# Casting DMAs on GpSimd's queue in place of casts on the engines, in an attention and MLP kernel

One core of a Trainium2 chip. The metric is the device time of one execution in microseconds (us), lower is better. A run more than 1.5% above the fastest of its kernel is called slow and left out of the ratios.

## The reference, cut to what matters

```python
# q, k, v: (4 batches, 8 heads, 768 positions, 64); n_sink = 4, window = 128
scores = q @ k.T / 8, kept where the key is one of the first 4 or within the window of 128
x   = softmax(scores) @ v                    # heads side by side: (4, 768, 512)
a1  = alpha1 * x + beta1
tok = w_tok @ a1                             # w_tok: (768, 768), over positions
u   = x + lam * tok
a2  = alpha2 * u + beta2
out = u + lam * (relu(a2 @ w_ch1) @ w_ch2)   # w_ch1: (512, 2048), w_ch2: (2048, 512)
```

All inputs are fp32; the products run in fp16.

## The kernel before

The program is a list of tasks. A planner in Python with estimated costs puts them in a fixed order on each engine and gives them buffers. Each engine then works through its own list in that order: a task that waits holds all that stand behind it. Batch 0's attention runs first, alone (the startup); then the MLP of batch b runs on TensorE beside the attention of batch b+1.

All loads are on SyncE's one queue, as fp32, and an engine casts each to fp16. A row below is one contiguous piece of the source; a load moves many of them:

```python
def load_qk(p, b, hp, t, wait=None):            # rows of 6 x 64 fp32 = 1536 bytes
    src = (q, k)[t][b, 2 * hp : 2 * hp + 2].rearrange("h (p r) d -> p h (r d)", p=P)
    done["nat", b, hp, t] = add(p, {SP: 480}, lambda e: nc.sync.dma_start(bf.t, src), ...)

def load_v0(p, G, r):                           # batch 0's v: rows of 64 fp32 = 256 bytes
    done["v0", G, r] = add(p, {SP: 520}, lambda e: nc.sync.dma_start(
        bf.t[:, sl], v[0, 4*G : 4*G+4, r*P : (r+1)*P, :].rearrange("h p d -> p h d")), ...)
# load_wtok: 6 loads with rows of 3072 bytes; load_w1, load_w2: rows of 2048 bytes into 4 staging buffers
...
# the order on SyncE's queue
for hp, t in QK_ORDER[:4]: load_qk(at(), 0, hp, t)
for r in range(2):         load_v0(at(), 0, r)
for hp, t in QK_ORDER[4:]: load_qk(at(), 0, hp, t)
... the rest of v0, then w_tok, w_ch1, lam, batch 1's q/k, w_ch2, batch 1's v
...
# casts: q/k on VectorE and GpSimd, v on GpSimd (one on ScalarE), w_tok on ScalarE and GpSimd,
# w_ch1 on ScalarE and GpSimd (8 each); w_ch2 is multiplied by lam on VectorE or GpSimd
# row sums of w_tok (for beta1): 36 small matmuls with a column of ones
```

The softmax here doesn't subtract the row's maximum and nothing guards it: scores larger than these inputs give would overflow.

## Time and profile before

| | before |
|---|---|
| median of three (lowest to highest) | 273.24 us (272.65 to 274.75) |
| span of the profiled run | 272.6 us |
| first MLP matmul of batch 0 | 44.0 us |
| first token product of batch 1 | 102.7 us |
| first MLP matmul of batch 1 | 112.4 us |

The three moments cut the run into a startup (44.0 us), the MLP stage of batch 0 (58.7), a gap in which batch 1's token product and its transposes run (9.7) and the rest (160.2). Each is the start of the first matmul of its group in TensorE's timeline (the prediction has the first at 43.8, read from the groups by window).

From the view of the DMA issues: how many loads of which size, and at the end the median us from issue to landing:

```profile
v<-in_v_dram SPq DMA_DIRECT2D x12, 128.0 KB, 4.7
```

From the page's 40 slices: the clock granted to TensorE in tenths (9 is 90% or more), never lowered.

```profile
PEclk9999999999999999999999999999999999999999
```

### The profile page before, as it was taken

How to read it: one execution, taken by the hardware profiler on the slowest of the kernel's cores; microseconds unless marked ns; L12 is line 12 of the kernel's file. 1: busy time of each engine (PE TensorE's matmuls, PEld its weight loads, DVE VectorE, ACT ScalarE, POOL GpSimd, SP SyncE). 2: the span in 40 equal slices, each digit the busy share in tenths (PEclk: the TensorE clock that was granted, in tenths of full speed). 3: DMA queues.
4: the chain of work that ended last, by engine and by line, in shares of the span. 5: the costliest groups of instructions: out<-in, count | busy, mean ns of one | idle time of the engine just before them, and what ended most of it. 6: DMA issues, size and time to landing. Idle time of an engine off the chain costs nothing.

```text
span 272.6 us, 4969 instructions
## 1 busy us (share of the span) xinstructions
PE 259.3 (95%) x1941; PEld 142.5 (52%) x1941; DVE 144.4 (53%) x292; ACT 129.9 (48%) x213; POOL 115.5 (42%) x139
## 2 busy tenths in 40 slices
PE   7799999996899999799999999999999999999994
PEld 7644756653454544355655444555654445665441
DVE  5565744776989925438895143379853333100222
ACT  1778936786741102688740024787700145773000
POOL 5649957820395895106988700004846000000000
PEclk9999999999999999999999999999999999999999
DMA  6999999999999536779978523100001223000221
GB/s 226 324 245 357 374 291 258 274 357 234 254 284 212 149 108 173 173 165 218 219 145 175 165 77 96 59 2 0 2 38 43 96 84 93 0 0 2 77 77 77
DMA packets 85838, 42.28 MB, mean 155 GB/s; under 512 B 73515, under 2 KB 77619, under 8 KB 85814
## 3 DMA queue, kind: packets, MB, share of 16 engines
q1 hardware_dynamic: 85792, 41.95, 57.4%
q8 instruction: 15, 0.25, 0.4%
q14 instruction: 9, 0.07, 0.1%
q10 hardware_dynamic: 22, 0.01, 0.0%
HBM read 30.16 MB, written 6.29 MB: 134 GB/s over the span
## 4 chain that ended last, share of the span: by engine, by line
PE 68%; DMA 17%; DVE 7%; SPq 4%; POOL 2%; issue 1%; ACT 1%; POOLq 0%; DVEq 0%; ACTq 0%
PE ch L808 29%; PE h L784 24%; PE tok L701 9%; DMA wst_w<-in_moe_w_ch_dram 6%; DMA nat<-in_q_dram 5%; DMA lb_b<-in_moe_beta_dram 3%; SPq L364 3%; DVE w2f L683 3%; PE pv L570 3%; PE S L523 2%; DVE E L547 2%; DMA wtn<-in_moe_w_tok_dram 2%; POOL w1f L228 1%; PE pv L563 1%; POOL n L228 1%
## 5 line engine op out<-in xcount | busy, mean ns | idle before, releaser
L784 PE MATMUL h<-uT,w1f 128*128 128x384 f16 x512 | 90.5, 326 | 2.7 <-DVE uT L730 1.5
L808 PE MATMUL ch<-w2f,hT 128*128 128x512 f16 x384 | 88.7, 379 | 0.5 <-DVE w2f L683 0.5
L784 PEld LDWEIGHTS <-w1f 128*128 128x128 f16 x512 | 47.7, 98 | 36.2 <-issue 7.0
L808 PEld LDWEIGHTS <-hT 128*128 128x128 f16 x384 | 36.3, 98 | 41.8 <-issue 1.4
L790 ACT ACTIVATE hT<-h 128x384 f16<-128x384 f32 x95 | 46.1, 492 | 19.9 <-PE h L784 18.2
L538 ACT ACTIVATE E<-S 128x1024 f16<-128x1024 f32 (+1 forms) x42 | 40.7, 1003 | 14.0 <-PE pv L570 8.6
L819 DVE TENSOR_TENSOR x<-x,ch 128x512 f32<-128x512 f32 x24 | 16.5, 686 | 52.2 <-PE ch L808 51.6
L612 POOL TENSOR_TENSOR tmp<-x,la_b 128x512 f32<-128x512 f32 x18 | 25.8, 1435 | 42.5 <-DVE x L594 42.4
L226 ACT CAST u<-x 128x512 f16<-128x512 f32 x20 | 12.3, 618 | 61.7 <-DVE x L710 61.7
L701 PE MATMUL tok<-xh,wtokT 128*128 128x512 f16 x144 | 34.4, 379 | 0.0
L228 POOL CAST n<-nat 128x768 f16<-128x768 f32 x28 | 25.2, 914 | 16.7 <-DMA nat<-in_q_dram 12.8
L710 DVE TENSOR_TENSOR x<-x,tok 128x512 f32<-128x512 f32 x24 | 16.4, 687 | 23.6 <-PE tok L701 18.6
L615 POOL TENSOR_TENSOR xh<-tmp,lb_b 128x512 f16<-128x512 f32 x18 | 25.0, 1389 | 0.7
L792 DVE TENSOR_SCALAR hT<-h 128x384 f16<-128x384 f32 x33 | 18.3, 554 | 11.4 <-PE h L784 11.0
L547 DVE TENSOR_TENSOR E<-E,maskn 128x1024 f16<-128x1024 f16 x25 | 24.2, 997 | 0.0
L701 PEld LDWEIGHTS <-wtokT 128*128 128x128 f16 x144 | 13.9, 98 | 16.1
L594 DVE TENSOR_TENSOR x<-pv,rec 128x256 f32<-128x256 f32 x48 | 20.4, 425 | 1.7
L570 PE MATMUL pv<-vf,E 128*128 128x65 f16 x328 | 18.2, 194 | 3.1 <-DVE E L547 2.2
L570 PEld LDWEIGHTS <-E 128*128 128x128 f16 x328 | 15.2, 97 | 9.3 <-DVE E L547 2.8
L683 DVE TENSOR_TENSOR w2f<-wst_w,lam_b 128x512 f16<-128x512 f32 x15 | 12.5, 870 | 3.6 <-DMA wst_w<-in_moe_w_ch_dram 3.5
L228 POOL CAST u<-x 128x512 f16<-128x512 f32 x4 | 2.5, 626 | 27.9 <-DVE x L710 27.9
L228 POOL CAST vf<-vnat 128x512 f16<-128x512 f32 x18 | 10.7, 616 | 7.7 <-DMA vnat<-in_v_dram 7.2
(94 smaller groups left out, 206.3 us busy)
## 6 DMA issues: line engine op xcount, KB each, us to landing
wst_w<-in_moe_w_ch_dram SPq DMA_DIRECT2D x16, 512.0 KB, 8.1
nat<-in_q_dram SPq DMA_DIRECT2D x16, 384.0 KB, 6.1
nat<-in_k_dram SPq DMA_DIRECT2D x16, 384.0 KB, 9.0
out_dram<-x SPq DMA_DIRECT2D x24, 256.0 KB, 2.0
vnat<-in_v_dram SPq DMA_DIRECT2D x18, 256.0 KB, 4.5
wtn<-in_moe_w_tok_dram SPq DMA_DIRECT2D x6, 384.0 KB, 5.7
v<-in_v_dram SPq DMA_DIRECT2D x12, 128.0 KB, 4.7
uT<-u SPq DMA_TRANSPOSE x18, 2.3
```

Of the source, the lines that this page charges most:

```text
L228: engine[e].tensor_copy(o, i)
L538: nc.scalar.activation(eT.t, pS.t[:, :, 0 : n * w].rearrange("p e (i w) -> p e i w", i=n), AF.Exp, scale=scale)
L547: nc.vector.tensor_mul(ev, ev, m.to_broadcast(list(ev.shape)))
L570: nc.tensor.matmul(po.t[:, hl, :], eT.t[:, e_, off + i, c : c + P], vf[j][:, h, :], start=(r < 2 and n == 0), stop=(n == len(parts) - 1 an ...
L594: nc.vector.tensor_mul(bx.t[:, 4 * G : 4 * G + 4, :], po.t[:, :, 0:D], rec.t.to_broadcast([P, 4, D]))
L612: nc.gpsimd.tensor_mul(tmp.t, bx.t.rearrange("p h d -> p (h d)"), la1_b)
L615: nc.gpsimd.tensor_add(bh.t, tmp.t, lb1_b)
L683: lambda e, a=a, src=src: engine[e].tensor_mul(w2f[:, a, :], src.t[:, a % 2, :], lam_b),
L701: nc.tensor.matmul(pt.t, wtokT[:, si, ti * P : (ti + 1) * P], hs[si].t, start=(si == 0), stop=(si == NR - 1 and b > 0))
L784: nc.tensor.matmul(ph.t, w1f[:, c, fi * P : (fi + 1) * P], bu.t[:, c, chk * NTOK : (chk + 1) * NTOK], start=(c == 0), stop=(c == NC - 1))
L790: nc.scalar.activation(bh.t[:, fi, :], ph.t, AF.Relu)
L808: nc.tensor.matmul(pc.t, bh.t[:, fi, nt * P : (nt + 1) * P], w2f[:, fi, :], start=(fi == 0), stop=(fi == NF - 1))
```

## The change

The intent: a DMA that GpSimd issues changes the type on the way. So q/k of batches 0 and 1, w_tok and w_ch1 arrive as fp16, and some 40 casts go. Row sums of w_tok become a reduction and a diagonal matrix, lam and beta1 are spread by small matmuls in place of broadcast loads, and the constants become planned tasks. SyncE's queue keeps v, w_ch2 and the later batches. The core of the diff:

```diff
+    def cast_qk(p, b, t, hps, wait=None):
+        src = (q, k)[t][b, 2*hps[0] : 2*hps[0] + n].rearrange("h (p r) d -> p h (r d)", p=P)
+        a = load(p, POOL, 530 + 50*n, lambda e: nc.gpsimd.dma_start(at_(bf)[:, lo:lo+n], src), ...)   # fp16 bf
     def load_wtok(p, ti, n):
-            nc.sync.dma_start(bf.t[:, ti % 3, :], moe_w_tok[ti*P : (ti+1)*P, :])
+            nc.gpsimd.dma_start(wt16.t[:, ti:ti+n, :], moe_w_tok[ti*P : (ti+n)*P, :]...)
     def load_w1(p, i):
-        for c in range(0, NC, 2): load_w(...)            # staging, cast later
+        nc.gpsimd.dma_start(w1f[:, :, i*512 : (i+1)*512], moe_w_ch1[:, i*512 : (i+1)*512]...)
...
-    for hp, t in QK_ORDER[:4]: load_qk(at(), 0, hp, t)   # and v0, w_tok, w_ch1 ..., all on SyncE
+    for hps in ((0,), (1,), (2, 3)):                     # on GpSimd's queue, first of all
+        for t in range(2): cast_qk(-10000 + 12*hps[0] + t, 0, t, hps)
+    g = gate(at(), done["c16", 0, 0, 0], ...)            # SyncE: after the first q piece
+    for G in range(2):
+        for r in range(NR): load_v0(at(), G, r, g)
+    for ti in range(0, NR, 2): load_wtok(-9000 + ti, ti, 2)
+    for i in range(2): load_w1(-8000 + 100*i, i)
+    ... batch 1's q/k (four casting DMAs), the other two of w_ch1
+    g = gate(at(), done["w1", 0], ...)
+    ... on SyncE: batch 1's v, w_ch2
```

GpSimd thus issues batch 0's q/k, w_tok, w_ch1 and batch 1's q/k without a break.

## The prediction

> **What bounds the kernel now.** I read four views, in this order. First the chain that ended last, in order of time:
>
> ```profile
> 1.81 5.61 DMA nat<-in_q_dram
> 7.44 0.37 SPq L337
> ...
> 31.48 9.19 DMA lb_b<-in_moe_beta_dram
> 40.72 0.09 issue
> 40.81 0.70 POOL lb_b L859
> 41.51 5.29 DMA wst_w<-in_moe_w_ch_dram
> 46.85 0.61 POOL w1f L228
> ...
> 58.12 6.67 DMA wst_w<-in_moe_w_ch_dram
> 64.81 1.29 DVE w2f L683 x2
> ...
> 227.21 20.80 PE h L784 x128
> 248.01 20.73 PE ch L808 x96
> 268.84 0.69 DVE x L819
> ```
>
> From about 85 us to 268.8 us the chain is TensorE alone: nothing that the change touches can shorten that stretch except by starting it earlier. Before 85 us it is DMA landings, casts on GpSimd and w2 products on VectorE. The chain's last stretch also gives the true price of a matmul: 20.80 us / 128 = 162.5 ns for 384 columns, 0.423 ns a column.
>
> Second, the groups by shape, with TensorE's counts in windows. PE's 95% busy hides waiting, so I multiplied the columns in each window by 0.423 ns (half for the half-array products S, a quarter for the sink products):
> - 0 to 43.8 us (the first MLP matmul starts there): 25.8 us of work, 18 us lost.
> - 43.8 to 102.85 us (MLP of batch 0 beside attention of batch 1): 52.0 us in 59.05, 7.0 lost, 4.9 of them between 60 and 80.
> - 170 to 227 us (the same stage, batch 2): 55.7 us in 57.0, 1.3 lost.
> So at most the 18 us and some 5.7 us are to be had.
>
> Third, durations of what goes and what stays:
>
> ```profile
> L228 POOL CAST n<-nat 128x768 f16<-128x768 f32 x28 | 25.2, 914 | 16.7 <-DMA nat<-in_q_dram 12.8 <-DVE w2f L683 2.6 <-DMA nat<-in_k_dram 1.2
> ...
> L683 DVE TENSOR_TENSOR w2f<-wst_w,lam_b 128x512 f16<-128x512 f32 x15 | 12.5, 870 | 3.6 <-DMA wst_w<-in_moe_w_ch_dram 3.5
> ...
> L603 POOL TENSOR_TENSOR xh<-x,la_b 128x256 f16<-128x256 f32 x12 | 8.5, 728 | 4.6 <-DVE rec L593 3.8 <-DVE x L594 0.5 <-PE S L523 0.2
> ...
> L228 POOL CAST w1f<-wst_w 128x512 f16<-128x512 f32 x8 | 4.9, 613 | 3.8 <-DMA wst_w<-in_moe_w_ch_dram 3.8
> L228 POOL CAST vf<-v 128x256 f16<-128x256 f32 x11 | 4.3, 408 | 0.8 <-DMA v<-in_v_dram 0.7
> ```
>
> Columns: count, busy us, mean ns, idle before. Fourth, the windows of 2 us, for the DMA's rate (last column, GB/s): q/k run at 300 to 360, the v loads with their 256-byte rows at about 210, w_tok and w_ch1 at 345 and more.
>
> ```profile
> 4.00:6.00 2.00, 2.00 (x22) 2.00 (x21) 1.57 (x3) 0.00 (x0) 0.59 (x2) 1.00 0.96 310
> ...
> 16.00:18.00 2.00, 2.00 (x22) 0.83 (x19) 1.05 (x2) 1.75 (x3) 0.87 (x3) 1.00 1.07 226
> ...
> 24.00:26.00 2.00, 2.00 (x29) 1.04 (x29) 0.56 (x2) 1.98 (x3) 1.82 (x5) 1.00 1.01 345
> ```
>
> The share of the DMA engines (the column before) is about 1 from 2 us on: in the first 40 us data comes as fast as it can, and a cast on the way doesn't lessen what is read.
>
> **What the Trainium skill says.** (1) "DMA: Bandwidth & Descriptors", Anatomy of one DMA: a GpSimd-issued transfer carries some 2.0 us of fixed cost. No run of before shows one; SP's first q load, issued at 0.80 us, is being cast at 3.95 us, so the first landing should differ little. (2) Same page, Queues, rings and completion order: the queues share the 16 engines, which take turns packet by packet. The trace agrees as to the sharing only in that one queue alone already fills the engines (share about 1). (3) "TensorEngine Tiling (Array Packing)", Key Properties and Restrictions: changing the tiling mode drains TensorE, and column tiling disables fast weight load. Before: eight S products take 0.54 us where their columns make 0.43, so a visit to another mode costs 0.1 us. (4) "SBUF — State Buffer", Who interferes with whom: VectorE in a two-port mode can starve GpSimd's descriptor writing. Not shown by before; most descriptors are written in the first 5 us, when VectorE only does memsets.
>
> **The change, part by part.**
> - *Casts gone.* 12 of the GpSimd n casts (0.82 us each, 9.9), 4 on VectorE (2.7), the six of w_tok (ACT 3.1, POOL 1.6), sixteen of w_ch1 (ACT 4.9, POOL 4.9). GpSimd loses 16.4 us, ScalarE 8.0. The 36 rs matmuls go too (36 x 128 columns, 1.9 us of PE), and the broadcast loads of lam and beta1, with the wait of 3.3 us on GpSimd for the latter.
> - *Added.* Row sums (three on ScalarE, three on VectorE, 0.8 us each by the cast of the same width), six small diagonals, one more spread copy.
> - *A new wait on GpSimd.* In the changed kernel's instruction order GpSimd issues fifteen DMAs ahead of any other work except the selects; from the ninth on each waits for the DMA eight earlier to land (they share eight semaphores; before shows SP held the same way, its load at 7.44 us released by the q landing at 7.42). The fifteenth waits for the seventh, the first w_tok piece. Call its landing T. Until T GpSimd casts no v, and PE in its fixed order stops at the sink-v product, ahead of the second head group's scores.
> - *T.* q/k of batch 0, 8 x 384 KB = 3.15 MB at 325 GB/s: 9.7 us; w_tok's first piece 0.79 MB at 350: 2.2 us; start about 2.3 us (estimate: first issue at 0.8 as in before, descriptors, first byte). That is 14.2. v of batch 0, 1.57 MB at 210, is 7.5 us and shares the engines from about 5 us on (it is held only until the first q piece). If it gets half the time or more it is all in front of T: 21.7. If it gets a small share, T is near 16. I take 19.
> - *From T to the MLP.* GpSimd: last issue 0.7, 11 v casts x 0.408 = 4.5, two row products x 1.25 = 2.5, 12 xh x 0.728 = 8.7: T + 16.4. ScalarE's second-group exps with three row sums among them end at about T + 12, so GpSimd leads. Then TensorE still has 34 of the 42 token matmuls x 0.216 us = 7.3. First MLP matmul at T + 24 = 43 us, against 43.8: the startup gains 0.8 us, not more, although so many casts went.
> - *MLP of batch 0.* w_ch1 needs no buffer and no cast; w_ch2's loads start when the first w_ch1 piece has landed (about T + 8), not after 47 us; VectorE does 10 rather than 15 of its products, and most before batch 1's masks. So the loss of 4.9 us between 60 and 80 should mostly go. Against it: the 8 q/k transposes of batch 1 are now 12 half-width matmuls each rather than 6. If column halves run side by side, as the four sink products do (0.33 us for what would be 0.87), that costs only drains, 4 visits x 0.1; if not, 8 x 0.33 = 2.7. I take 1.7. Batch 1's second half of q/k waits for buffers, so its scores start after 28 of 32 MLP-1 tiles rather than 17; I leave 1.5 us of stall. 52.0 + 1.3 + 1.7 + 1.5 = 56.5, against 59.05: 2.5 us gained.
> - *After.* Batches 1 to 3 keep their work: 0.
> Sum: -0.8 - 2.5 = -3.3 us: 273.2 becomes about 269.5 (rounded down a little, since GpSimd's freed time should help somewhere).
>
> **Rivals.** (A) The new queue takes v's place: T near 15 to 16, startup gains 4 us, half-width transposes are free, stalls gone: 264. For it: v's rows are 256 bytes, q's 1536, so turns taken descriptor by descriptor favour q. Against: turns may be by larger packets. (B) GpSimd becomes the bound of the startup: T at 22, first MLP matmul at 46, and what the MLP stage gains is just given back: 272 to 274. For it: the sum above needs only the v loads ahead of w_tok. (C) Casting transfers move slower than plain ones: 10% on the 5.5 MB ahead of T is 1.5 us, half the rate 12 us: up to 282. Nothing in the trace speaks for it; none is there to look at. (D) The late start of batch 1's attention leaves GpSimd's xh (6 x 2.8 us) and 8 casts (7.3 us) too little time before the token product: about 24 us from 72 us on, to 96, where TensorE arrives at about 100. Narrow; 1 to 3 us if missed.
>
> **Range and chances.** T moves the result one for one between 16 and 22 (-4 to +2 about the middle), the MLP stage by 2 either way: 263.5 to 275.5. Over 2% faster means under 267.8, which needs A at least in part: 0.38. Slower by 2% needs C: 0.07. The rest, 0.55, is within 2%.
>
> **What would show it.** Right: GpSimd idle until the first w_tok piece lands, then busy without a gap; its last half-width xh 16 us later; first MLP matmul near T + 24; almost no waits for w2 between 60 and 80; the wait of ScalarE or PE in 10 to 25 us put to GpSimd or v. Wrong: GpSimd free well ahead of the w_tok landing, a slow rate (under 300 GB/s) while only the casting queue runs, transposes of 0.66 us, or PE idle before batch 1's token product.

## The result and the profile after

| | before | after |
|---|---|---|
| median (lowest to highest) | 273.62 us (272.65 to 274.75) | 287.69 us (286.43 to 290.53) |
| span of the profiled run | 272.6 us | 288.5 us |
| startup | 44.0 | 60.2 |
| MLP stage of batch 0 | 58.7 | 53.9 |
| gap | 9.7 | 13.5 |
| rest | 160.2 | 160.9 |

The changed kernel is slower: ratio 1.053, 95% interval 1.044 to 1.062, four runs each. (A ratio is the mean time of one kernel's fast runs over that of the other's of the same rounds, so not quite the ratio of the medians.) The profiled run of after is the slowest of its four; its 15.9 us over before are +16.2 in the startup, -4.8 in the MLP stage, +3.8 in the gap and +0.7 in the rest.

The startup's loss is in one place. The DMA issues of after, first with the casting loads of w_ch1, then with v:

```profile
w1f<-in_moe_w_ch_dram POOLq DMA_DIRECT2D x4, 512.0 KB, 20.1
v<-in_v_dram SPq DMA_DIRECT2D x12, 128.0 KB, 13.6
```

The same twelve loads of 128 KB take a median of 13.6 us to land where they took 4.7, and since only some can be under way at a time, SyncE needed from 5.9 to 38.4 us to issue them (by 16.6 before). The chain that ended last, up to the first MLP matmul:

```profile
5.93 0.77 SPq L391
...
20.82 19.16 DMA v<-in_v_dram
39.98 0.05 issue
40.03 0.40 POOL vf L233
40.43 2.05 POOL xh L628 x3
...
60.37 1.79 PE h L799 x11
```

The chain goes from one issue of v to the next, then through a v landing at 40 us, and from there through GpSimd's last casts and products to TensorE. In before this part of the chain was v's issues up to 16.6 us and then w_tok (`17.24 5.25 DMA wtn<-in_moe_w_tok_dram`). The waits between 14 and 62 us (total us, times, longest) say who stood still for it:

```profile
POOL vf L233 <- DMA v<-in_v_dram: 15.9, 6, 4.2
ACT vf L231 <- DMA v<-in_v_dram: 10.3, 1, 10.3
```

In before GpSimd's casts of v waited 0.7 us in all (the tile view of v: who waited for it, us, times):

```profile
  POOL vf L228: 0.7, 1
```

ScalarE had one v cast in its list and stood before it for 10.3 us, with the exponentials behind it. GpSimd's own new wait, which the prediction was about, ended early. Its timeline (start, us, line, what, idle before and the releaser):

```profile
18.59 0.74 POOL L419 DMA_DIRECT2D w1f<-in_moe_w_ch_dram  x1 [1.51 <-DMA wt<-in_moe_w_tok_dram]
...
33.65 0.40 POOL L233 CAST vf<-v 128x256 f16<-128x256 f32 x1 [4.19 <-DMA v<-in_v_dram]
36.63 0.40 POOL L233 CAST vf<-v 128x256 f16<-128x256 f32 x1 [2.58 <-DMA v<-in_v_dram]
40.03 0.40 POOL L233 CAST vf<-v 128x256 f16<-128x256 f32 x1 [3.00 <-DMA v<-in_v_dram]
```

The last held issue is at 18.6 us, on w_tok's first landing; after it the engine is idle, not busy. The clock row shows TensorE idling too, at half clock around 30 us:

```profile
PEclk9997568999999999977999999999999999999998
```

What the two queues did can be counted from the trace's DMA records, which hold one record for each row. In 2-us bins from about 15.4 to 37.4 us of the span (counted from the records themselves, some 4-byte ones among them; q0 is the casting queue, q1 SyncE's with v):

```
q0 rows  237  241  264  306  308  319  373  396  368  318  318
q1 rows  241  240  260  308  300  324  367  363  364  323  317
q0 GB/s  169  174  166  157  151  155  147  147  147  156  157   (bytes written; twice that is read)
q1 GB/s   30   29   33   38   37   40   46   45   46   40   40
```

Row for row the two queues are served alike here, whatever the rows hold. The casting rows are 3072, 2048 or 1536 bytes at the source, v's are 256. So v moved at 29 to 46 GB/s for 22 us while data that nobody needed yet (w_tok until 22 us, then w_ch1 and half of batch 1's q/k) took the rest. When the casting queue ran dry at about 40 us, the rows of v (soon batch 1's) went from 31 to 18 ns each. Read rates added, the DMA engines moved some 340 to 380 GB/s throughout, on average as much as in before (352 and 348 GB/s from 16.5 to 38.5 us): no bandwidth was lost, only the order.

The time of one row also shows the price of casting: 1536 bytes take 65 ns plain (batch 0's q/k in before) and 79 ns cast, 3072 bytes 121 and 134, 2048 bytes 84 and 96. So 12 to 14 ns, 11 to 22%.

### The profile page after: what moved, and what is told of

Same layout as the page of the kernel before. It is cut to its first block, busy times and chain, and to the rows that moved or that the text cites. A ratio compares the mean times of both kernels' runs of the same rounds, so it can differ in the third digit from the quotient of the medians.

```text
span 288.5 us, 5023 instructions
## 1 busy us (share of the span) xinstructions
PE 268.5 (93%) x2000; PEld 144.1 (50%) x2000; DVE 136.4 (47%) x281; ACT 130.7 (45%) x214; POOL 116.8 (40%) x137
## 4 chain that ended last, share of the span: by engine, by line
PE 76%; DMA 11%; SPq 5%; POOL 4%; DVE 1%; issue 1%; ACT 0%; DVEq 0%; POOLq 0%
PE h L799 30%; PE ch L823 28%; PE tok L716 8%; DMA v<-in_v_dram 7%; SPq L391 5%; PE pv L595 3%; PE S L547 3%; DMA uT<-u 2%; POOL xh L628 2%; DMA c<-in_q_dram 1%; DMA qkT<-n 1%; PE pv L588 1%; PE tp L466 1%; POOL vf L233 1%; PE uTp L760 1%
## 5 line engine op out<-in xcount | busy, mean ns | idle before, releaser
L799 PE MATMUL h<-uT,w1f 128*128 128x384 f16 x512 | 91.9, 333 | 0.7 <-DVE uT L745 0.6
L805 ACT ACTIVATE hT<-h 128x384 f16<-128x384 f32 x98 | 48.0, 490 | 22.8 <-PE h L799 22.3
L563 ACT ACTIVATE E<-S 128x1024 f16<-128x1024 f32 (+1 forms) x42 | 40.9, 1002 | 10.8 <-PE S L547 7.2
L637 POOL TENSOR_TENSOR tmp<-x,la_b 128x512 f32<-128x512 f32 x18 | 24.7, 1372 | 39.8 <-DVE x L619 39.3
L834 DVE TENSOR_TENSOR x<-x,ch 128x512 f32<-128x512 f32 x24 | 16.5, 688 | 50.0 <-PE ch L823 49.4
L725 DVE TENSOR_TENSOR x<-x,tok 128x512 f32<-128x512 f32 x24 | 16.4, 687 | 23.7 <-PE tok L716 18.4
L807 DVE TENSOR_SCALAR hT<-h 128x384 f16<-128x384 f32 x30 | 16.6, 554 | 14.1 <-PE h L799 13.9
L595 PE MATMUL pv<-vf,E 128*128 128x65 f16 x328 | 20.0, 200 | 2.9 <-POOL vf L233 2.9
L572 DVE TENSOR_TENSOR E<-E,maskn 128x1024 f16<-128x1024 f16 x25 | 22.3, 921 | 0.0
L595 PEld LDWEIGHTS <-E 128*128 128x128 f16 x328 | 16.9, 101 | 10.0 <-issue 5.1
L233 POOL CAST u<-x 128x512 f16<-128x512 f32 x5 | 3.4, 688 | 38.4 <-DVE x L725 38.4
L233 POOL CAST n<-nat 128x768 f16<-128x768 f32 x16 | 13.5, 852 | 13.2 <-DMA nat<-in_q_dram 8.1
L618 DVE RECIPROCAL rec<-pv 128x4 f32<-128x4 f32 x48 | 8.5, 178 | 12.9 <-PE pv L595 12.8
L547 PE MATMUL S<-qkT 64*128 64x256 f16 (+1 forms) x168 | 14.2, 281 | 0.0
## 6 DMA issues: line engine op xcount, KB each, us to landing
v<-in_v_dram SPq DMA_DIRECT2D x12, 128.0 KB, 13.6
```

Source lines behind the costliest of these rows:

```text
L233: engine[e].tensor_copy(o, i)
L547: nc.tensor.matmul(pv_[:, e_, i, :], o.t[rows, 2 * hp + 1, j * P : (j + 1) * P], o.t[rows, 2 * hp, j * P : j * P + w], start=not bias, sto ...
L563: nc.scalar.activation(eT.t, pS.t[:, :, 0 : n * w].rearrange("p e (i w) -> p e i w", i=n), AF.Exp, scale=scale)
L572: nc.vector.tensor_mul(ev, ev, m.to_broadcast(list(ev.shape)))
L595: nc.tensor.matmul(po.t[:, hl, :], eT.t[:, e_, off + i, c : c + P], vf[j][:, h, :], start=(r < 2 and n == 0), stop=(n == len(parts) - 1 an ...
L637: nc.gpsimd.tensor_mul(tmp.t, bx.t.rearrange("p h d -> p (h d)"), la1_b)
```

## The experiments

Five theories: (1) turns row by row starve v; (2) GpSimd, held by its fifteen issues, is late; (3) SyncE's queue ranks behind GpSimd's, or the sharing is by bytes; (4) casting is slow; (5) the fall of TensorE's clock costs the time. The moments of all kernels, from their profiled runs:

| kernel | ratio to before (95%) | startup | MLP stage | gap | rest | v: median us to landing |
|---|---|---|---|---|---|---|
| before | 1 | 44.0 | 58.7 | 9.7 | 160.2 | 4.7 |
| after | 1.053 (1.044 to 1.062) | 60.2 | 53.9 | 13.5 | 160.9 | 13.6 |
| e1 wide rows of v | 1.002 (0.992 to 1.011) | 50.3 | 53.6 | 9.9 | 159.8 | 10.6 |
| e2 v first | 1.009 (1.004 to 1.015) | 49.5 | 54.0 | 11.0 | 160.5 | 3.0 |
| e3 GpSimd free | 1.048 (1.041 to 1.054) | 58.9 | 53.2 | 9.9 | 160.2 | 12.1 |
| e4 clock kept | 1.083 (1.078 to 1.089) | 61.4 | 57.2 | 16.9 | 158.4 | 13.5 |
| e5 two queues for v | 1.068 (1.064 to 1.072) | 62.3 | 55.6 | 11.1 | 160.8 | 11.6 and 11.9 |
| e6 w_ch1 alone | 1.030 (1.027 to 1.033) | 43.3 | 66.3 | 9.7 | 160.3 | 5.5 |
| e7 late casting | 1.039 (1.036 to 1.043) | 44.2 | 60.3 | 19.8 | 158.0 | 4.1 |
| e8 w_ch1 alone, reordered | 1.087 (1.083 to 1.092) | 43.5 | 72.4 | 20.8 | 158.1 | 5.3 |
| e9 early block | 1.006 (1.002 to 1.010) | 48.2 | 54.1 | 10.6 | 160.4 | 4.5 |
| e10 split block | 1.007 (1.003 to 1.012) | 46.4 | 57.7 | 9.9 | 160.0 | 4.8 |

### e1_wide_v: v in few wide rows

Its output is wrong, which doesn't matter for the time. Each partition gets other positions; sizes and bytes are right.

```diff
-  12 loads: v[0, 4*G : 4*G+4, r*P : (r+1)*P].rearrange("h p d -> p h d")            # rows of 256 bytes
+   4 loads: v[0, 4*G+2*i : 4*G+2*i+2].rearrange("h (p r) d -> p h (r d)", p=P)      # rows of 1536 bytes
   (each cast of v becomes two of half the width: 0.29 us each in place of 0.40)
```

> The changed kernel, but batch 0's v is read in rows of 1536 bytes (four loads) instead of 256 (twelve loads): same bytes, a sixth of the packets. The rows land in another order, so batch 0's result is wrong on purpose. Theory 1 (the two queues take turns one packet for one packet, so v's 256-byte rows get a small share of the bytes while the casting queue has work): v lands after about 1,024 turns of some 140 ns on 16 engines, all of it by 17 to 19 us instead of 40; the startup gets back 12 to 16 us and the time is 271 to 277 us. Theory 2 (GpSimd is held by its own queue of issues): GpSimd still leaves its last issue at 19 us, so v's casts start then, as in the changed kernel; the time stays above 284. Theory 3 (SP's queue simply ranks behind GpSimd's, or the engines share by bytes): v's landing doesn't depend on its row length, and the time stays above 284.

276.41 us median (272.05 to 280.38; two of the four runs slow), ratio of fast runs 1.002. The startup fell from 60.2 to 50.3 us. The view of the DMA issues:

```profile
v<-in_v_dram SPq DMA_DIRECT2D x4, 384.0 KB, 10.6
```

All of v, issued between 5.7 and 8.0 us, was in by 22 us (17 to 19 was expected); the row counts of the two queues were again equal (casting queue and SyncE's, in 2-us bins from 12 to 18 us: 241 and 243, 211 and 209, 185 and 186). The same bytes beside the same traffic, in a sixth of the rows, land 20 us earlier (the last landing of v in after is at 42 us): theory 1 is confirmed, 2 and 3 in the form expected here (no gain) are refuted. Of the 6 us that the startup still lacks, two delays are seen: v's larger share pushed w_tok's first landing, and so GpSimd's last held issue, from 18.6 to 20.8 us, and the two fp32 spread products right after it took 2.1 us at half clock.

### e2_hold: v first, the rest later

```diff
+  two one-element copies on GpSimd that need v's last loads of both groups; w_tok, w_ch1 and
+  batch 1's q/k are issued behind them
```

> The changed kernel, but GpSimd issues w_tok, w_ch1 and batch 1's q/k only after all of batch 0's v has landed (a one-element copy from v's last piece stands before them on GpSimd). Theory 1: v shares only with q/k of batch 0 and is all there at about 21 us; w_tok then takes until about 32 us, the first MLP matmul comes at 44 to 47 us instead of 60, the time is 272 to 277. Theory 2 (GpSimd held too long): GpSimd is now held until about 26 us instead of 19, so the time is as in the changed kernel or longer, 287 or more. Theory 4 (casting transfers are slow): w_tok and w_ch1 come later than before, so nothing is won: 285 or more.

275.92 us (275.37 to 276.81), ratio 1.009, the result correct; v landed in 3.0 us:

```profile
v<-in_v_dram SPq DMA_DIRECT2D x12, 128.0 KB, 3.0
```

GpSimd was done with its issues at 30.1 us here, 10.8 us later than in after, and yet the kernel was 12 us faster. That refutes theory 4 as the main cause: the same casting loads were made, and later. It is no clean test of theory 2, since GpSimd cast eight of the twelve pieces of v ahead of these issues (from 15.5 us on); e1 and e3 are. The startup was later than expected (49.5, not 44 to 47), and the chain shows where: the next load with 256-byte rows, batch 1's v, now stood beside the casting queue.

```profile
35.98 14.53 DMA vnat<-in_v_dram
```

### e3_free_pool: GpSimd let go early, the traffic the same

```diff
-  w_tok in three casting DMAs, w_ch1 in four
+  w_tok in one, w_ch1 in two      # the last issue is over by 12.5 us in place of 19.3
```

> The changed kernel with the same bytes on the casting queue in the same order, but w_tok as one DMA and w_ch1 as two: eleven casting DMAs instead of fifteen, so GpSimd waits only for the first three and is free at about 13 us instead of 19. Theory 2: the startup gains about 6 us, the time is 281 to 283. Theory 1: v still lands at about 40 us, so first MLP matmul stays at 58 to 62 us and the time at 285 to 290.

286.24 us (284.56 to 287.72), ratio 1.048. The tile view of v: GpSimd's first cast is 4 us earlier than in after, but the last is at 42.6, and it waits for v as before:

```profile
L233 POOL CAST vf<-v x12: 397/402/408, 15.0 to 42.6; 128x256 f16<-128x256 f32 x12
...
  POOL vf L233: 19.4, 6
```

The 285 to 290 of theory 1 holds. Taking away the new wait on GpSimd, the centre of the prediction, gained 1.4 us (287.69 less 286.24), which is inside the noise: the intervals of the two ratios overlap.

### e4_keep_clock: dummy products where TensorE stood idle

```diff
+  110, 36, 20 and 20 dummy products ahead of the second group's scores, some more ahead of w_tok's transposes
```

> The changed kernel with some 240 dummy products in the places where TensorE stood idle between 26 and 50 us, so that its granted clock, which fell to 0.5 there, may stay at 1. Theory 5 (the fall of the clock is what costs): most of the 16 us come back, 273 to 278. Theory 1: v sets the pace; only the turns of w_tok and what else ran at half clock are faster, 0 to 3 us: 284 to 289.

296.19 us (294.48 to 296.93), ratio 1.083. The first dummies held the clock at full from 30 to 60 us (0.66 from 20 to 30):

```profile
PEclk9996999999999999985999999999999999999999
```

and the startup still took 61.4 us. Alone this does not refute theory 5, because the dummies stood in the way: in this run the chain that ended last goes through TensorE without a break from 22 us on, and 11.2 us of it are dummies.

```profile
26.19 6.93 PE dummy L564 x110
35.49 2.01 PE dummy L564 x36
```

The trace of after limits the theory better. There the chain reaches 40 us through landings of v, whatever TensorE's clock; from 40 to 60 us TensorE was busy for 18 us at clocks of 0.84 and 0.94, which makes an estimated 1.9 us lost (7.75 x 0.16 + 10.2 x 0.06). So the clock is not the main cause; what it cost exactly no run shows. The time missed its range upward: the planner's order changed with the dummies, and the two later stages came out longer (MLP stage 57.2, gap 16.9).

### e5_two_v_queues: half of v on a third queue

```diff
-  nc.sync.dma_start(v ..., G = 1)
+  nc.scalar.dma_start(v ..., G = 1)        # ScalarE's own queue
```

> The changed kernel, but the six loads of batch 0's v for the second group of heads are issued by ScalarE on its own DMA queue, the other six stay on SyncE's; same rows of 256 bytes, same bytes. It tells whose turns the turns are. If every queue has its own turn, v now gets two packets of three: its 6144 rows need only some 3072 casting packets beside them. In the changed kernel the 34 us from 5.9 to 40 us held 6144 of each; by the measured packet times (31 ns a v row, about 100 a casting row) v's share of that is 0.24, so an estimate of 34 x (0.5 x 0.76 + 0.24) = 21 us: v has landed at about 27 us, the first MLP matmul is at 47 to 52 us in place of 60.4 and the time 275 to 281 us. If the turns are between the casting (software) side and the hardware queues taken together, nothing moves: v by 40 us, 285 to 290 us. If ScalarE is held by its issues (they would be 0.5 us each or wait), its first copies of q/k come later and the first scores with them: seen as an idle ScalarE before 15 us.

292.04 us (291.6 to 293.38), ratio 1.068: the time is a miss. The count is not. In 2-us bins from 17.5 to 27.5 us of the span (q0 casting, q1 SyncE, q10 ScalarE):

```
q0  219  224  270  279  276
q1  213  223  272  277  272
q10 217  226  271  278  274
```

One to one to one: in this run each queue has its own turn, hardware or software. The Trainium skill, "DMA: Bandwidth & Descriptors", Queues, rings and completion order, says so (a round of turns between the queue rows that have work, SyncE's and ScalarE's each a row of its own), and this trace agrees. v thus had two rows of three while both its queues had loads. But ScalarE's issues had to wait for semaphores of earlier loads, and the engine stood still for them:

```profile
ACT ks L231 <- DMA v<-in_v_dram: 20.6, 1, 20.6
```

v was complete at about 38 us (the last rows on ScalarE's queue start at 37.9) rather than 27, and ScalarE's first exponentials began only at 29.1 us. What v's extra turns won, the held engine lost; this was the last clause of the expectation.

### e6_w1_cast: the kernel before with w_ch1 alone cast, late

```diff
 (before)
-  w_ch1: eight loads on SyncE into staging buffers, 16 casts
+  w_ch1: four casting DMAs on GpSimd that need v's last load, straight into place
```

> The kernel before, with one part of the change only: w_ch1 comes by four casting DMAs of GpSimd, held until the last v load of batch 0 has landed; nothing else is cast by DMA. Gone: eight w_ch1 loads on SyncE's queue and their 16 casts (ScalarE 4.9 us, GpSimd 4.9); added: four issues of 0.74 us on GpSimd. Since the casting queue starts only when v is in, the theory of turns expects no late v: last v landing as before, first MLP matmul at 44 to 46 us (43.8 before, up to 1.5 us of issues more among the GpSimd products). The MLP of batch 0 should take 54 to 57 us in place of 59.05, as w_ch2 no longer waits for staging buffers: 268 to 272 us. If a casting queue costs by itself, wherever it stands (casting slow, GpSimd held), the first MLP matmul is at 48 us or later and the time 275 us or more. If the gain of the MLP stage came from batch 1's q/k casts and not from w_ch1, the stage stays at 58 to 59 us and the time at 272 to 275.

282.04 us (281.03 to 282.53), ratio 1.030, where 268 to 272 was expected. The startup is right, 43.3 us: a casting queue that starts when v is in does not hurt it. The loss comes after it, in TensorE's timeline:

```profile
43.33 2.76 PE L781 MATMUL h<-uT,w1f 128*128 128x384 f16 x16
45.93 0.28 PE L742 MATMUL uTp<-iden,u 128*128 128x128 f16 x2
57.62 0.61 PE L742 MATMUL uTp<-iden,u 128*128 128x128 f16 x4 [11.42 <-POOL u L232]
```

TensorE waited 11.4 us for a copy on GpSimd, and GpSimd stood, six tasks (7 us) ahead of that copy, in front of a product with the beta1 broadcast:

```profile
POOL lb_b L856 <- DMA lb_b<-in_moe_beta_dram: 9.3, 1, 9.3
```

It is the same thing once more. A load at the back of SyncE's queue, which now shares every turn (in 2-us bins from 32 to 40 us the two queues count 225 and 226, 214 and 211, 218 and 219, 215 and 218 rows), lands 15.6 us after its issue, 9.2 in before, and a list in fixed order makes an unrelated task wait for it.

### e8_w1_cast_b: that order mended

```diff
+  product of the beta1 broadcast not before 62 us of the plan, products of w_ch2 not before 56 us
+  copies of u of batch 0 on ScalarE only
```

> e6_w1_cast again with three fixes of its instruction order only: the product of the beta1 broadcast, the products of w_ch2 and the fp16 copies of u no longer stand on GpSimd and VectorE where they wait for late loads. In e6 the first MLP matmul came at 43.3 us as foreseen, but then GpSimd waited 9.3 us for the beta1 broadcast, in order ahead of a copy of u, and PE stood idle for 11.4 us. If that wait is the whole loss of e6 (282.0), the time is now 268 to 272 us, with the first MLP matmul at 43 to 45 us and no PE wait over 3 us between 44 and 80 us. If the wait is only replaced by another late load (everything behind the four early w_ch1 transfers lands later, since the casting queue takes every second packet from batch 1's q/k, w_ch2 and v), PE still loses 5 us or more between 44 and 80 us and the time is 274 to 280.

296.96 us (294.9 to 298.66), ratio 1.087: the second branch, and worse. The beta1 wait was gone, but now GpSimd stood 12.0 us before batch 1's v, ahead of a q/k cast that TensorE needed:

```profile
58.66 0.82 PE L438 MATMUL tp<-iden,n 128*128 128x128 f16 x6 [6.29 <-POOL n L232]
```

and the products of w_ch2, pushed back by hand, filled VectorE where batch 1's masks were due (stage 72.4, gap 20.8). The run shows only that the next late load takes the place of the one avoided; what w_ch1 alone is worth stays open.

### e7_late_casting: the change without its first 20 us

```diff
 (after)
-  casting DMAs for batch 0's q/k and for w_tok
+  plain loads on SyncE and casts on the engines, in the order of before
-  w_ch1 and batch 1's q/k: casting DMAs from 11 us on
+  the same, but needing v's last load of batch 0
```

> The changed kernel in all but its first 20 us: batch 0's q/k and w_tok come by plain loads on SyncE's queue and are cast by engines as in the kernel before; w_ch1 and batch 1's q/k stay casting DMAs, held until the last v load of batch 0 has landed. Row sums and constants stay as in the change. The theory of turns expects v as in the kernel before, the first MLP matmul at 44 to 47 us and, as in the changed kernel, an MLP stage of batch 0 of 53 to 55 us and a rest of 159 to 162: 266 to 271 us, the fastest of all kernels so far. If the loss of the changed kernel came from casting batch 1's data too (rows of v of batch 1 stand beside them), the token product of batch 1 waits and the time is 273 us or more.

284.56 us (283.28 to 285.32), ratio 1.039. The expected 266 to 271 is missed by far. But the startup is 44.2 us, within 0.2 of before: so the row sums, the planned constants and the half-width transposes together cost nothing there, and the 16.2 us belong to how and when the data are loaded. The loss is later: batch 1's q/k now came too late (11 to 12 us from issue to landing, the second half issued at 49.6 and 56.7 us), its attention slipped to the end of the MLP stage, and the gap grew to 19.8 us with TensorE busy for 15.15 of them at a clock of 0.82 (window view; the first pair of columns after the window is TensorE's):

```profile
104.40:124.20 19.80, 15.15 (x121) 7.67 (x120) 14.82 (x28) 13.49 (x18) 13.21 (x13) 0.82 1.10 206
```

### e9_early_block and e10_split_block: looking for a version that wins

```diff
 (e7)
+  four buffers for batch 1's fp16 q/k in place of two, six fp32 staging buffers in place of eight
+  w_ch2 asked for ahead of batch 1's v, copies of u on ScalarE, w_ch2's products not before 50 us
+  e9:  all eight casting DMAs as soon as the first v loads of the second group are in
+  e10: three of them from 24 us, five behind the startup's products on GpSimd
```

> e7_late_casting with batch 1's q/k cast transfers issued in one block with w_ch1's as soon as the first two v loads of the second group have landed (four buffers for them in place of two, paid by six staging buffers in place of eight), copies of u on ScalarE only, w_ch2's products not before 50 us. In e7 the first MLP matmul came at 44.2 us, but batch 1's q/k landed 12 us after their late issue, the attention of batch 1 slipped behind the MLP, and TensorE's gap between batch 1's token product and its first MLP matmul grew from 9.7 to 19.8 us. If lateness of batch 1's q/k is the cause, that gap is back at 9 to 13 us and the time is 266 to 272 us, with the first MLP matmul at 44 to 49 us (eight issues of 0.75 us now stand among GpSimd's products, and w_tok shares its packets). If the transfers themselves are the limit (the casting queue's turns make batch 1's v or w_ch2 late), the time stays at 275 us or more.

> e9_early_block with its eight casting DMAs in two places: the first quarter of w_ch1 and half of batch 1's q/k at about 23 us, when all of v has landed, the other five behind the products of the startup on GpSimd, at about 35 us. In e9 the stage from the first MLP matmul to batch 1's token product took 54.1 us (59.05 before) and the gap after it 10.6 us, but the first MLP matmul came at 48.2 us, 4 us later than in e7 (44.2), because eight issues of 0.75 us and the casting rows stood in front of w_tok and the last products. If that is so, the first MLP matmul is now at 44 to 45.5 us, the stage takes 54 to 56 us and the time is 269 to 272.5 us, 0.5 to 1.5% faster than before. If the late half of batch 1's q/k misses its attention as in e7, the stage takes 58 us or more or the gap 14 us or more, and the time is 274 us or above.

e9: 274.78 us (273.87 to 275.78), ratio 1.006. e10: 275.8 us (274.6 to 276.92), ratio 1.007. TensorE's first MLP matmuls, e9 and then e10:

```profile
48.17 2.11 PE L808 MATMUL h<-uT,w1f 128*128 128x384 f16 x12
```

```profile
46.39 2.76 PE L808 MATMUL h<-uT,w1f 128*128 128x384 f16 x16
```

e9 has the short stage (54.1) and a normal gap (10.6), and pays 4.2 us in the startup for it; e10 pays 2.4 there and has a stage of 57.7. Both miss their range by about 3 us and neither beats the kernel before. No version tried does.

## Why the prediction was wrong, point by point

- *T, GpSimd's release: right, in part by luck.* 19 us predicted; the last held issue began at 18.6. But 19 was picked between 16 and 21.7 without a rule for the sharing, and the first casting load took 3.9 us from issue to landing where the first load of before took 3.1. And e3, which let GpSimd go 6.8 us earlier, gained 1.4 us, inside the noise: this wait was not what mattered.
- *"From T to the MLP": the step that failed.* It counts "11 v casts x 0.408 = 4.5" and the products behind them from T on, as if all of v lay ready at T. The duration was right (0.40), the data was not there: GpSimd waited 15.9 us for v after T, the last half-width product ended at 50.1 us, T + 31.5 in place of T + 16.4, and the first MLP matmul came at 60.2 in place of 43.
- *Rival A had the mechanism and the wrong sign.* It said that the new queue takes v's place if turns are taken descriptor by descriptor, and counted that as a gain, "T near 15 to 16". The question asked of v was only how much it delays T, never when v itself lands. With the rule of equal turns the answer was at hand: 6144 rows of v need 6144 casting rows beside them. Batch 0's q/k and w_tok have 2048 and 768 of those, so v was still on its way during most of w_ch1 (2048) and the half of batch 1's q/k that comes early (1024). The new kernel's planner has a like error: where both queues have work it gives each an equal share of the time (`both / 2`) and not of the rows; what that did to the order of the tasks no run shows.
- *MLP of batch 0: the direction right, the size too small.* 2.5 us of gain predicted, 4.8 in the profiled run, and e1, e2 and e9 show 4.6 to 5.1 too. The stall that it named did go: TensorE was idle for 4.0 us of this stage in before (3.3 of them between 60 and 80 us), and for 0.15 in after (window views). One term that was too dear is "I take 1.7" for the half-width transposes: in the timeline twelve of them take 0.53 us where the six full-width ones of before take 0.50 to 0.51.
- *"After: 0": mis-sized.* The gap grew by 3.8 us, the rest by 0.7. Rival D, "1 to 3 us" for late xh (the products of x with alpha1) on GpSimd, fits only a part: TensorE waited 0.9 us for xh in the gap and 2.2 for an exponential. The cause of the rest stays open. It is not the late start as such: e3 and e5 start their MLP at 58.9 and 62.3 us and have gaps of 9.9 and 11.1.
- *Rival C.* A casting row takes 11 to 22% longer than a plain one. The rival's "half the rate" did not happen; alone, from 4 to 8 us, the casting queue read 319 GB/s in after and 344 in e2.

The sum as measured: +16.2 - 4.8 + 3.8 + 0.7 = +15.9 us between the profiled runs, where -3.3 was predicted. (These are single profiled runs, and the four runs of after lie within 4.1 us, so shares are good to some us.) Shown by runs: v's late landing, through equal turns by rows, is worth about 10 of the 16 us in the startup (e1: 9.9; e2, which changes GpSimd's order too: 10.7); and casting queues placed after v cost the startup nothing (e6, e7). Not settled: the other 5 to 6 us. e1 and e2 each have a wait of their own there, GpSimd's release and batch 1's v, and no run takes away both. Open too is whether some order keeps both the old startup and the short MLP stage; together they would make an estimated span of 268 us (272.6 less 4.8).

## What to carry to other kernels

Before moving loads to a second DMA queue, list for each queue its rows and not its bytes: while both had work in these runs they advanced row for row, so a load with narrow rows that is needed soon goes at the rate of its neighbour's wide rows. Put it first, or let the second queue start when it has landed. And in a kernel with a fixed order on each engine, work out when each piece of data lands, not only when the engine is free: a saved cast is worth nothing if the engine then stands before an empty buffer.

## What the Trainium skill lacked or had wrong

- "DMA: Bandwidth & Descriptors", Queues, rings and completion order: it has the turns between queues by packets of several descriptors, and this agrees as to equal turns (241 to 240 rows; 276 to 272 to 274 with three queues). It lacks the consequence: the rate of a queue with short rows is set by the row length of its neighbours (v at 29 to 46 GB/s beside 147 to 174 written, and back to 18 ns a row from 31 when alone). Whether a turn is one row or several in a run was not resolved by these counts.
- The same page, SWDGE vs HWDGE vs iDMA, says that casting needs GpSimd's queue, and gives no price. Here a casting row took 79 ns for 65 plain (1536 bytes), 96 for 84 (2048 bytes) and 134 for 121 (3072 bytes).
